# A state recurrence and a dense feed-forward layer on one core: 512 instead of 256 tokens per step of the layer

## The chip, the core and the metric

The kernel runs on one core of a Trainium2 chip. The core has a matrix engine (TensorE, PE in the profile; PEld is its weight load), VectorE (DVE), ScalarE (ACT), GpSimd (POOL) and SyncE (SP), which here only issues DMAs. Each engine works through its own instructions in the order in which they were written; the engines wait for one another on semaphores. Matmuls write to PSUM, eight banks of 2 KB per partition; all else lies in SBUF or in memory (HBM). The metric is the device time of one execution in microseconds.

## What is computed

```python
def _attn_ref(r, k, v, w, a, b):            # 4 batches, 8 heads, 768 steps, 40 wide
    for t in range(S):
        y[:, :, t] = np.einsum('bhd,bhde->bhe', rt, state)
        Sa = np.einsum('bhde,bhe->bhd', state, at)
        state_decay = state * wt[:, :, None, :] - np.einsum('bhd,bhe->bhde', Sa, bt)
        state = state_decay + np.einsum('bhd,bhe->bhde', vt, kt)

def _moe_ref(x, w_in, w_out):               # x: 3072 tokens x 320; w_in 320 x 2048; w_out 2048 x 320
    h = x @ w_in
    sp = np.where(h > 20.0, h, np.log1p(np.exp(np.minimum(h, 20.0))))
    g = h * np.tanh(sp)
    return (g @ w_out).astype(np.float32)
```

The recurrence's output y, reordered to 3072 tokens of 320 numbers, is the x of the dense layer.

## The kernel before

The first part (`attention`) computes the recurrence in 12 chunks of 64 time steps. Each chunk gives 256 tokens, which go to memory as `yD`, together with a factor `pD`; a token's x is the product of the two. A step of a chunk has parts a, u, d, b and c for each of two groups g of heads; part a's products are L284, part b's L314 with a mask on VectorE (L316), part c's L334 and L339 with a VectorE update of the state (L342, L346) and a ScalarE copy of the result (L343).

The second part (`Mlp.run`) is the dense layer. It takes T = 256 tokens at a time, one chunk, in 12 rounds i. Both products are made exact enough by splitting each factor into a rounded part (xh, gh and the weights' w_ih, w_oh) and its remainder (xl, gl, w_il, w_ol), in the type fp32r:

- `load_x(i)`: eight DMAs from SyncE's queue (four of `yD` into xy, L472 and L475; four of `pD` into xp, L473 and L476), then VectorE multiplies the two (L565), ScalarE rounds (xh, L566), VectorE subtracts (xl, L567, and L568). xy and xp have one buffer each (NXP = 1), xh and xl two (NX = 2).
- `mlp1(i, q)`, q = 0..3: a quarter of the 2048 hidden rows, as two PSUM banks ph of 2 blocks of 128 rows x 256 tokens; each block takes eight matmuls (L583). ScalarE applies the activation to a bank (L585) and then rounds all four blocks (gh, L588), VectorE subtracts (gl, L589). Four banks hold ph (NH = 4).
- `mlp2(i, q)`: 24 matmuls of 320 columns (L603 to L605): for each of four blocks of hidden rows and two blocks of 128 tokens, three matmuls into the token block's PSUM bank po. After q = 3 ScalarE copies each po to SBUF (os, L609) and SyncE's queue stores it (L610). Two of the four po banks are in use in a round; os has two buffers.

`mlp2` runs three quarters behind `mlp1` (LAG = 3), so that TensorE alternates between 32 matmuls of the first product and 24 of the second. The second weight matrix is read and split (`cv_d`, `cv_m`, `cv_w`: L453 to L463, L494, L495) in eight parts, three before the dense layer and five (`third`) after its first quarter.

The order of each engine's instructions is made by a list scheduler from priorities. It lets the dense layer's first instructions slip in between the last two steps of the recurrence (chunks 10 and 11), where TensorE would wait.

Of the kernel before, what the change touches and what calls it, by code (L numbers as in the profile page):

```python
# [7 lines left out]
F32 = mybir.dt.float32  # L8
F32R = mybir.dt.float32r
AF = mybir.ActivationFunctionType  # L10
# [33 lines left out]
def at(tc, k):  # L44
    return tc.high_priority(offset=OFF[k]) if OFF.get(k) else nullcontext()
# [33 lines left out]
def attention(ctx, tc, I, yD, pD, nch, M):  # L79
# [143 lines left out]
    def post_inv(n, TT, T1):  # L223
        gp = GP[n]
        for h in range(2):
            with at(tc, 'T%d' % h):
                px = ps_a.tile([64, 16, 32], F32, name="pa")
# [200 lines left out]
NHB = 3  # L428
NGB = 6
# [49 lines left out]
class Mlp:  # L479
# [70 lines left out]
    def run(self, nsc):  # L550
        tc, nc, W, yD, pD, out = self.tc, self.tc.nc, self, self.yD, self.pD, self.out
        V, A, PE, SP, G = nc.vector, nc.scalar, nc.tensor, nc.sync, nc.gpsimd
        T = 256
        ps_h, mpa = self.ps_h, self.mpa
        mp = self.pool("mp", 2, "left")
        ps_o = self.pool("ps_o", 8 - NH, "left", space=PSUM)

        def load_x(i):
            y = self.mpx.tile([128, 3, T], F32, name="xy", bufs=NXP)
            p = self.mpx.tile([128, 3, T], F32, name="xp", bufs=NXP)  # L560
            load_yp(nc, i, yD, pD, y, p, True)

            xh = self.mpx.tile([128, 3, T], F32R, name="xh", bufs=NX)
            xl = self.mpx.tile([128, 2, T], F32R, name="xl", bufs=NX)
            V.tensor_tensor(out=y, in0=y, in1=p, op=ALU.mult)  # L565
            A.copy(xh, y)  # L566
            V.tensor_tensor(out=xl, in0=y[:, 0:2], in1=xh[:, 0:2].bitcast(F32), op=ALU.subtract)  # L567
            V.tensor_tensor(out=xh[64:128, 2], in0=y[64:128, 2], in1=xh[64:128, 2].bitcast(F32), op=ALU.subtract)  # L568
            return xh, xl

        def mlp1(q, xh, xl):
            g = mpa.tile([128, 4, T], F32, name="g", bufs=NHB)
            for f0 in (0, 2):
                ph = ps_h.tile([128, 2, T], F32, name="ph")
                for j in range(2):
                    f = slice((f0 + j) * 128, (f0 + j) * 128 + 128)
                    o = ph[:, j]

                    for n, (w, x) in enumerate(((W.ih[q][:, 0, f], xh[:, 0]), (W.ih[q][:, 0, f], xl[:, 0]),
                                                (W.ih[q][:, 1, f], xh[:, 1]), (W.ih[q][:, 1, f], xl[:, 1]),  # L580
                                                (W.il[q][:, 0, f], xh[:, 0]), (W.il[q][:, 1, f], xh[:, 1]),
                                                (W.ih[q][:, 2, f], xh[:, 2]), (W.il[q][:, 2, f], xh[:, 2]))):
                        PE.matmul(o, w, x, start=(j == 0 and n == 0), stop=(n == 7), skip_group_check=True)  # L583

                A.activation(g[:, f0:f0 + 2], ph, AF.Mish)  # L585
            gh = mp.tile([128, 4, T], F32R, name="gh", bufs=NGB)
            gl = mp.tile([128, 4, T], F32R, name="gl", bufs=NGB)
            A.copy(gh, g)  # L588
            V.tensor_tensor(out=gl, in0=g, in1=gh.bitcast(F32), op=ALU.subtract)  # L589
            return gh, gl  # L590

        pos = {}

        def mlp2(i, q, gh, gl):
            if q == 0:
                pos[i] = [ps_o.tile([128, 320], F32, name="po") for _ in range(2)]
            po = pos[i]
            for j in range(4):
                f = q * 4 + j
                for k in range(2):  # L600
                    t = slice(k * 128, k * 128 + 128)
                    oh, ol = (w[f // 2][:, f % 2 * 320:f % 2 * 320 + 320] for w in (W.oh, W.ol))
                    PE.matmul(po[k], gh[:, j, t], oh, start=(f == 0), stop=False, skip_group_check=True)  # L603
                    PE.matmul(po[k], gh[:, j, t], ol, start=False, stop=False, skip_group_check=True)  # L604
                    PE.matmul(po[k], gl[:, j, t], oh, start=False, stop=(f == 15), skip_group_check=True)  # L605
            if q == 3:
                for k in range(2):
                    o = mp.tile([128, 320], F32, name="os")
                    A.copy(o, po[k])  # L609
                    SP.dma_start(out=out[i * T + k * 128:i * T + k * 128 + 128], in_=o)  # L610

        wait = []
        x = load_x(0)
        for i in range(nsc):
            for q in range(4):
                wait.append((i, q) + mlp1(q, *x))
                if (i, q) == (0, 0):
                    self.third()
                if q == 1 and i + 1 < nsc:
                    nx = load_x(i + 1)  # L620
                if len(wait) > LAG:
                    mlp2(*wait.pop(0))
            x = nx
        for w in wait:
            mlp2(*w)
# [32 lines left out]
```

## Time and profile before

| | us |
|---|---|
| median of 3 runs (lowest to highest) | 829.57 (829.17 to 835.69) |
| the profiled execution | 826.83 |
| its span, first to last instruction | 825.1 |
| TensorE busy in the span | 724.1 (88%) |
| VectorE, ScalarE, GpSimd busy | 461.1, 428.6, 103.2 |

The span is the profiled execution without some 1.7 us around it. Busy shares are means over two very different parts: a recurrence up to about 478 us, where the engines wait for each other, and the dense layer behind it. A row of a timeline gives the start, the duration, the engine, the line, the operation with its output and inputs, and in brackets how long the engine stood idle before it and who released it. A matmul's duration contains its way through the array, which overlaps the next one; how fast matmuls follow one another is read from their starts.

### The profile page before, as it was taken

The numbers are of one execution on the slowest core, as the hardware profiler recorded it, in microseconds if no ns is written. First come the engines' busy times: TensorE is split into PE (matmuls) and PEld (weight loads), VectorE is DVE, ScalarE is ACT, GpSimd is POOL, SyncE is SP. The second block draws the span as 40 slices with busy tenths as digits, with TensorE's granted clock in tenths as the row PEclk, the third lists the DMA queues.
The fourth block names the chain that finished last, engine by engine and source line by source line (L and its number), as shares of the span: only waits on it lengthen the run. The fifth ranks groups of instructions, "written<-read, shape, count | busy, mean of one in ns | idle before, by whom it ended". The sixth has DMA issues, their size and how long they took to land.

```text
span 825.1 us, 18795 instructions
## 1 busy us (share of the span) xinstructions
PE 724.1 (88%) x7816; PEld 679.3 (82%) x7816; DVE 461.1 (56%) x975; ACT 428.6 (52%) x937; POOL 103.2 (13%) x182
## 2 busy tenths in 40 slices
PE   2544798999789889889886999999999999999998
PEld 1433687788788788778775899999999999999998
DVE  6789979748989758889846456222222122122110
ACT  5534658775485866666784556233333333333331
POOL 8100021223222023221102100000000000000000
PEclk9767889999989999999999999999999999999999
DMA  6522323334433233423328543121121112000000
GB/s 174 143 73 65 96 54 73 93 82 111 106 84 81 60 97 103 92 74 111 105 92 191 130 139 99 39 56 33 23 55 37 36 39 55 18 20 17 17 1 33
DMA packets 58213, 61.92 MB, mean 75 GB/s; under 512 B 25536, under 2 KB 48704, under 8 KB 58128
## 3 DMA queue, kind: packets, MB, share of 16 engines
q1 hardware_dynamic: 49296, 40.94, 17.7%
q0 software_dynamic: 8832, 19.79, 9.9%
q8 instruction: 61, 1.00, 0.5%
q14 instruction: 24, 0.20, 0.1%
HBM read 48.79 MB, written 11.86 MB: 74 GB/s over the span
## 4 chain that ended last, share of the span: by engine, by line
PE 51%; ACT 9%; DVE 8%; DMA 4%; issue 2%; SPq 0%; DVEq 0%; ACTq 0%
PE ph L583 21%; PE po L604 7%; PE po L605 7%; PE po L603 7%; PE pa L258 3%; DMA cv_d<-in_wo 2%; PE pa L186 2%; DVE tmp L214 1%; DVE XL L216 1%; ACT bdT L249 1%; ACT bdT L250 1%; PE pq L314 1%; ACT KT L260 1%; PE pu L284 1%; DMA cv_d<-in_wi 1%
## 5 line engine op out<-in xcount | busy, mean ns | idle before, releaser
L583 PE MATMUL ph<-xh,w_ih 128*128 128x256 f32 x576 | 148.3, 283 | 3.1 <-ACT xh L566 3.1
L585 ACT ACTIVATE g<-ph 128x512 f32<-128x512 f32 x96 | 57.3, 598 | 180.0 <-PE ph L583 179.9
L589 DVE TENSOR_TENSOR gl<-g,gh 128x1024 fp32r<-128x1024 f32 x48 | 58.6, 1225 | 159.1 <-ACT gh L588 158.8
L583 PE MATMUL ph<-xh,w_il 128*128 128x256 f32 x576 | 123.7, 283 | 0.0
L186 PE MATMUL pa<-bk,ad 128*128 128x168 f32 x384 | 80.6, 359 | 45.5 <-DVE bk L170 15.0
L604 PE MATMUL po<-w_ol,gh 128*128 128x320 f32 x384 | 118.7, 309 | 0.1
L605 PE MATMUL po<-w_oh,gl 128*128 128x320 f32 x384 | 118.4, 309 | 0.0
L603 PE MATMUL po<-w_oh,gh 128*128 128x320 f32 x384 | 117.9, 309 | 0.0
L583 PEld LDWEIGHTS ph<-xh,w_ih 128*128 128x128 f32 x576 | 109.3, 190 | 3.4 <-ACT xh L566 3.4
L186 PEld LDWEIGHTS pa<-bk,ad 128*128 128x128 f32 x384 | 67.0, 222 | 50.8 <-issue 22.8
L583 PE MATMUL ph<-xl,w_ih 128*128 128x256 f32 x384 | 100.9, 284 | 0.0
L583 PEld LDWEIGHTS ph<-xh,w_il 128*128 128x128 f32 x576 | 96.2, 190 | 0.1
L583 PEld LDWEIGHTS ph<-xl,w_ih 128*128 128x128 f32 x384 | 73.1, 190 | 0.5 <-issue 0.3
L604 PEld LDWEIGHTS po<-w_ol,gh 128*128 128x128 f32 x384 | 72.1, 188 | 0.5 <-DVE w_ol L495 0.5
L605 PEld LDWEIGHTS po<-w_oh,gl 128*128 128x128 f32 x384 | 72.1, 188 | 0.1
L603 PEld LDWEIGHTS po<-w_oh,gh 128*128 128x128 f32 x384 | 71.8, 188 | 0.2
L216 DVE TENSOR_TENSOR XL<-XL,tmp 128x30 f32<-128x30 f32 (+9 forms) x180 | 59.0, 328 | 2.4
L214 DVE TENSOR_TENSOR tmp<-XL 128x30 f32<-128x30 f32 (+9 forms) x180 | 58.6, 325 | 2.3
L258 PE MATMUL pa<-bdT,HA 128*104 128x128 f32 x384 | 52.3, 291 | 6.9 <-ACT bdT L251 5.7
L258 PEld LDWEIGHTS pa<-bdT,HA 128*104 128x104 f32 x384 | 47.3, 182 | 10.6 <-ACT bdT L251 7.4
L314 PE MATMUL pq<-bdr,UVT 128*128 128x128 f32 x384 | 53.7, 285 | 0.3 <-DVE UVQ L316 0.2
L588 ACT CAST gh<-g 128x1024 fp32r<-128x1024 f32 x48 | 50.1, 1048 | 1.1
(89 smaller groups left out, 1219.6 us busy)
## 6 DMA issues: line engine op xcount, KB each, us to landing
wa<-in_wa SPq DMA_DIRECT2D x48, 162.5 KB
bk<-in_bk SPq DMA_DIRECT2D x48, 160.0 KB
cv_d<-in_wi SPq DMA_DIRECT2D x12, 512.0 KB
cv_d<-in_wo SPq DMA_DIRECT2D x8, 640.0 KB
pD<-P POOLq DMA_DIRECT2D x48, 81.2 KB, 2.2
VS<-in_vN POOLq DMA_DIRECT2D x24, 160.0 KB, 3.5
UVT<-in_vD POOLq DMA_DIRECT2D x24, 160.0 KB, 4.4
bdr<-in_rD POOLq DMA_DIRECT2D x24, 160.0 KB, 4.4
```

The source lines that it names most:

```text
L186: PE.matmul(pt[:, j], ad[:, s0 + j].rearrange("p k a t -> p (k a t)"), bk[:, s0 + j], start=(j == 0), stop=True, skip_group_check=True)
L214: V.tensor_tensor(out=tv, in0=X[:, i + 1:32, i:i + 1].broadcast_to([128, 31 - i, i]), in1=X[:, i:i + 1, 0:i].broadcast_to([128, 31 - i, i] ...
L216: V.tensor_tensor(out=X[:, i + 1:32, 0:i], in0=X[:, i + 1:32, 0:i], in1=tv, op=ALU.add)
L258: PE.matmul(pk[:, j], ha[:, s0 + j], bd[:, s0 + j].rearrange("p a t -> p (a t)"), start=(j == 0), stop=True, skip_group_check=True)
L314: PE.matmul(pq[:, s], UVT[:, g * 4 + s, be * 128:be * 128 + 128], br[:, be, g * 4 + s].rearrange("p a t -> p (a t)"), start=(s == 0), stop ...
L583: PE.matmul(o, w, x, start=(j == 0 and n == 0), stop=(n == 7), skip_group_check=True)
L585: A.activation(g[:, f0:f0 + 2], ph, AF.Mish)
L588: A.copy(gh, g)
L589: V.tensor_tensor(out=gl, in0=g, in1=gh.bitcast(F32), op=ALU.subtract)
L603: PE.matmul(po[k], gh[:, j, t], oh, start=(f == 0), stop=False, skip_group_check=True)
L604: PE.matmul(po[k], gh[:, j, t], ol, start=False, stop=False, skip_group_check=True)
L605: PE.matmul(po[k], gl[:, j, t], oh, start=False, stop=(f == 15), skip_group_check=True)
```

## The change

T becomes 512: a round i of the dense layer takes two chunks, and there are six rounds of eight steps q (`range(nsc // 2)`, `range(8)`). Line numbers behind the load move by one or two (L583 becomes L584, L585 L586, L609 L610, L565 L567).

- `load_x` issues the DMAs of two chunks (16) into tiles of twice the width, and then one multiply, one rounding and two subtractions on twice the columns.
- `mlp1` computes an eighth of the hidden rows: two blocks of 128 rows, each a bank ph of 512 tokens by eight matmuls of 512 columns. g, gh and gl keep their size (2 x 512 in place of 4 x 256).
- `mlp2` takes two blocks of hidden rows and four token blocks: again 24 matmuls of 320 columns, into four po banks at once. All four banks are in use in a round, and at its end four po are copied through the two os buffers.
- The second product needs one part of the split second weight matrix per step, where it needed two.

```diff
--- before.py
+++ after.py
@@ -550,7 +550,7 @@
     def run(self, nsc):
         tc, nc, W, yD, pD, out = self.tc, self.tc.nc, self, self.yD, self.pD, self.out
         V, A, PE, SP, G = nc.vector, nc.scalar, nc.tensor, nc.sync, nc.gpsimd
-        T = 256
+        T = 512
         ps_h, mpa = self.ps_h, self.mpa
         mp = self.pool("mp", 2, "left")
         ps_o = self.pool("ps_o", 8 - NH, "left", space=PSUM)
@@ -558,7 +558,9 @@
         def load_x(i):
             y = self.mpx.tile([128, 3, T], F32, name="xy", bufs=NXP)
             p = self.mpx.tile([128, 3, T], F32, name="xp", bufs=NXP)
-            load_yp(nc, i, yD, pD, y, p, True)
+            for c in range(2):
+                t = slice(c * 256, c * 256 + 256)
+                load_yp(nc, 2 * i + c, yD, pD, y[:, :, t], p[:, :, t], True)
 
             xh = self.mpx.tile([128, 3, T], F32R, name="xh", bufs=NX)
             xl = self.mpx.tile([128, 2, T], F32R, name="xl", bufs=NX)
@@ -569,22 +571,21 @@
             return xh, xl
 
         def mlp1(q, xh, xl):
-            g = mpa.tile([128, 4, T], F32, name="g", bufs=NHB)
-            for f0 in (0, 2):
-                ph = ps_h.tile([128, 2, T], F32, name="ph")
-                for j in range(2):
-                    f = slice((f0 + j) * 128, (f0 + j) * 128 + 128)
-                    o = ph[:, j]
-
-                    for n, (w, x) in enumerate(((W.ih[q][:, 0, f], xh[:, 0]), (W.ih[q][:, 0, f], xl[:, 0]),
-                                                (W.ih[q][:, 1, f], xh[:, 1]), (W.ih[q][:, 1, f], xl[:, 1]),
-                                                (W.il[q][:, 0, f], xh[:, 0]), (W.il[q][:, 1, f], xh[:, 1]),
-                                                (W.ih[q][:, 2, f], xh[:, 2]), (W.il[q][:, 2, f], xh[:, 2]))):
-                        PE.matmul(o, w, x, start=(j == 0 and n == 0), stop=(n == 7), skip_group_check=True)
-
-                A.activation(g[:, f0:f0 + 2], ph, AF.Mish)
-            gh = mp.tile([128, 4, T], F32R, name="gh", bufs=NGB)
-            gl = mp.tile([128, 4, T], F32R, name="gl", bufs=NGB)
+
+            g = mpa.tile([128, 2, T], F32, name="g", bufs=NHB)
+            for j in range(2):
+                ph = ps_h.tile([128, T], F32, name="ph")
+                f = slice((q % 2 * 2 + j) * 128, (q % 2 * 2 + j) * 128 + 128)
+                h, l = W.ih[q // 2], W.il[q // 2]
+
+                for n, (w, x) in enumerate(((h[:, 0, f], xh[:, 0]), (h[:, 0, f], xl[:, 0]), (h[:, 1, f], xh[:, 1]),
+                                            (h[:, 1, f], xl[:, 1]), (l[:, 0, f], xh[:, 0]), (l[:, 1, f], xh[:, 1]),
+                                            (h[:, 2, f], xh[:, 2]), (l[:, 2, f], xh[:, 2]))):
+                    PE.matmul(ph, w, x, start=(n == 0), stop=(n == 7), skip_group_check=True)
+
+                A.activation(g[:, j], ph, AF.Mish)
+            gh = mp.tile([128, 2, T], F32R, name="gh", bufs=NGB)
+            gl = mp.tile([128, 2, T], F32R, name="gl", bufs=NGB)
             A.copy(gh, g)
             V.tensor_tensor(out=gl, in0=g, in1=gh.bitcast(F32), op=ALU.subtract)
             return gh, gl
@@ -593,30 +594,30 @@
 
         def mlp2(i, q, gh, gl):
             if q == 0:
-                pos[i] = [ps_o.tile([128, 320], F32, name="po") for _ in range(2)]
+                pos[i] = [ps_o.tile([128, 320], F32, name="po") for _ in range(4)]
             po = pos[i]
-            for j in range(4):
-                f = q * 4 + j
-                for k in range(2):
+            for j in range(2):
+                f = q * 2 + j
+                oh, ol = (w[f // 2][:, f % 2 * 320:f % 2 * 320 + 320] for w in (W.oh, W.ol))
+                for k in range(4):
                     t = slice(k * 128, k * 128 + 128)
-                    oh, ol = (w[f // 2][:, f % 2 * 320:f % 2 * 320 + 320] for w in (W.oh, W.ol))
                     PE.matmul(po[k], gh[:, j, t], oh, start=(f == 0), stop=False, skip_group_check=True)
                     PE.matmul(po[k], gh[:, j, t], ol, start=False, stop=False, skip_group_check=True)
                     PE.matmul(po[k], gl[:, j, t], oh, start=False, stop=(f == 15), skip_group_check=True)
-            if q == 3:
-                for k in range(2):
+            if q == 7:
+                for k in range(4):
                     o = mp.tile([128, 320], F32, name="os")
                     A.copy(o, po[k])
                     SP.dma_start(out=out[i * T + k * 128:i * T + k * 128 + 128], in_=o)
 
         wait = []
         x = load_x(0)
-        for i in range(nsc):
-            for q in range(4):
+        for i in range(nsc // 2):
+            for q in range(8):
                 wait.append((i, q) + mlp1(q, *x))
                 if (i, q) == (0, 0):
                     self.third()
-                if q == 1 and i + 1 < nsc:
+                if q == 3 and i + 1 < nsc // 2:
                     nx = load_x(i + 1)
                 if len(wait) > LAG:
                     mlp2(*wait.pop(0))
```

How this moves instructions is shown at three places. In all of them ph, xh, xl, w_ih and w_il are the tiles of the first product; pu, pq, KT, VS, UVQ, ST and bkn are those of the recurrence.

TensorE, before, where the first matmuls of the dense layer stand: in part c of chunk 10, between the two halves of group 0 (L334, L339).

```order
L334 MATMUL pq<-UVQ_119,bkn 64x104
L334 MATMUL pq<-UVQ_120,bkn 64x104
L339 MATMUL pq<-bdr_121,smd 64x2x64 x4
L583 MATMUL ph<-xh,w_ih_927 128x256 x2
L583 MATMUL ph<-xh,w_ih_5064 128x256 x2
L334 MATMUL pq<-UVQ_119,bkn 64x104
```

TensorE, after, at the first matmuls of the dense layer: they stand behind all of chunk 10's part c and just ahead of chunk 11's part a for group 1 (L284, L304).

```order
L334 MATMUL pq<-UVQ_120,bkn 64x104
L339 MATMUL pq<-bdr_121,smd 64x2x64 x4
L584 MATMUL ph<-xh,w_ih_927 128x512 x4
L284 MATMUL pu<-KT,VS_116 64x64
L304 MATMUL pu<-cst,ST_123 128x128 x4
L284 MATMUL pu<-KT,VS_116 64x64 x7
L284 MATMUL pu<-KT,VS_117 64x64 x8
L584 MATMUL ph<-xl,w_ih_927 128x512
L584 MATMUL ph<-xh,w_ih_927 128x512
L584 MATMUL ph<-xl,w_ih_927 128x512
```

So the first matmuls of the dense layer move behind three halves of part c and one part a, and four of them stand ahead of the other part a.

VectorE, before, around the multiply of the first x (L565), in part c of chunk 10: the state updates L342 and the split of the second weight matrix (cv_w, w_ol) follow it.

```order
L316 TENSOR_TENSOR UVQ_119<-pq,cst 128x8x64
L461 TENSOR_SCALAR cv_w<-cv_m 128x640
L565 TENSOR_TENSOR xy<-xy,xp 128x768
L462 SCALAR_TENSOR_TENSOR cv_w<-cv_m,cv_w 128x640
L342 TENSOR_TENSOR stn<-ST_122,pq 128x160
L463 SCALAR_TENSOR_TENSOR cv_w<-cv_d,cv_w 128x640
L567 TENSOR_TENSOR xl<-xy,xh 128x512
L568 TENSOR_TENSOR xh<-xy,xh 64x256
L495 SCALAR_TENSOR_TENSOR w_ol_5371<-cv_w,w_oh_5370 128x640
L342 TENSOR_TENSOR stn<-ST_122,pq 128x160
```

VectorE, after, at the same multiply (L567 now), first place: it stands between the two updates (L342) of group 1's state ST_123.

```order
L346 TENSOR_TENSOR ST_122<-stn,R 128x8x40
L495 SCALAR_TENSOR_TENSOR w_ol_5371<-cv_w,w_oh_5370 128x640
L342 TENSOR_TENSOR stn<-ST_123,pq 128x160
L567 TENSOR_TENSOR xy<-xy,xp 128x1536
L342 TENSOR_TENSOR stn<-ST_123,pq 128x160
L346 TENSOR_TENSOR ST_123<-stn,R 128x8x40
L569 TENSOR_TENSOR xl<-xy,xh 128x1024
```

VectorE, after, at the multiply of the second x: it stands between the third and the fourth mask product (L316) of chunk 11's part b.

```order
L316 TENSOR_TENSOR UVQ_120<-pq,cst 128x8x64
L316 TENSOR_TENSOR UVQ_119<-pq,cst 128x8x64
L567 TENSOR_TENSOR xy<-xy,xp 128x1536
L316 TENSOR_TENSOR UVQ_120<-pq,cst 128x8x64
L569 TENSOR_TENSOR xl<-xy,xh 128x1024
L570 TENSOR_TENSOR xh<-xy,xh 64x512
L590 TENSOR_TENSOR gl<-g,gh 128x1024 x4
```

What moved: both multiplies are twice as wide, and an instruction of the recurrence that the next matmuls need now stands right behind each.

ScalarE, before, at the end of a round, with the semaphores that each instruction waits for (DMAHW: a DMA; 49 is only a label): two copies of po to os between two roundings and activations.

```order
L588 CAST gh<-g 128x1024 [waits Activation_49]
L609 COPY os<-po 128x320 [waits DMAHW1_49,PE_49]
L609 COPY os<-po 128x320 [waits DMAHW2_49,PE_49]
L585 ACTIVATE g<-ph 128x512 [waits DVE_49,PE_49]
L585 ACTIVATE g<-ph 128x512 [waits PE_49]
L566 CAST xh<-xy 128x768 [waits DMAHW5_49,DMAHW6_49,DMAHW4_49,DMAHW3_49]
```

ScalarE, after, at the end of a round: four copies, the third and the fourth of which wait for a DMA more.

```order
L589 CAST gh<-g 128x1024 [waits Activation_49]
L610 COPY os<-po 128x320 [waits PE_49] x2
L610 COPY os<-po 128x320 [waits DMAHW5_49,PE_49,Activation_49]
L586 ACTIVATE g<-ph 128x512 [waits DVE_49,PE_49]
L610 COPY os<-po 128x320 [waits DMAHW6_49,Activation_49]
L586 ACTIVATE g<-ph 128x512 [waits PE_49]
L589 CAST gh<-g 128x1024 [waits Activation_49]
```

What moved: the third copy stands ahead of the next activation (L586) and waits until the first copy's buffer has been stored; the fourth stands behind that activation.

## Rows read from the trace of the kernel before

**Rows 1.** The page's head and TensorE's line; share of the span in brackets.

```profile
span 825.1 us, 18795 instructions
...
PE 724.1 (88%) x7816; PEld 679.3 (82%) x7816; DVE 461.1 (56%) x975; ACT 428.6 (52%) x937; POOL 103.2 (13%) x182
```

**Rows 2.** TensorE by stretch: window, its length, busy us (matmuls), granted clock, DMA share, GB/s.

```profile
391.10:394.50 3.40, 1.70 (x49) 0.96 0.48 144
394.50:397.90 3.40, 3.40 (x19) 0.54 0.80 199
447.15:450.28 3.13, 0.00 (x0) 1.00 0.41 105
450.28:475.00 24.72, 24.00 (x287) 1.00 0.54 131
525.00:800.00 275.00, 275.00 (x2098) 1.00 0.11 30
```

**Rows 3.** Chain that ended last, in time: start us, us, engine, tile, line, count.

```profile
439.86 7.25 DMA cv_d<-in_wo
...
464.53 5.98 DMA xy<-yD
470.63 0.96 DVE xy L565
471.59 0.61 DVE UVQ L316
...
516.80 3.83 PE ph L583 x32
...
803.72 3.83 PE ph L583 x32
```

**Rows 4.** Timeline, lead-in: start us, us, engine, line, operation [idle before <-releaser].

```profile
446.54 0.61 PE L339 MATMUL pq<-bdr,smd 128*64 128x128 f32 x8
447.19 0.77 ACT L459 ACTIVATE cv_m<-cv_d 128x640 f32<-128x640 f32 x1 [4.46 <-DMA cv_d<-in_wo]
...
450.28 0.74 PE L583 MATMUL ph<-xh,w_ih 128*128 128x256 f32 x4 [3.14 <-ACT xh L566]
...
455.92 0.33 PE L284 MATMUL pu<-KT,VS 104*64 104x64 f32 x2 [0.54 <-ACT VS L277]
...
457.84 0.38 PE L583 MATMUL ph<-xh,w_ih 128*128 128x256 f32 x1
...
458.74 0.93 PE L334 MATMUL pq<-UVQ,bkn 128*64 128x104 f32 x16
...
459.94 0.88 PE L334 MATMUL pq<-UVQ,bkn 128*64 128x104 f32 x16
```

**Rows 5.** Groups by line and shape from 470 us: busy us, mean ns, idle before.

```profile
L589 DVE TENSOR_TENSOR gl<-g,gh 128x1024 fp32r<-128x1024 f32 x48 | 58.6, 1225 | 159.1 <-ACT gh L588 158.8
...
L588 ACT CAST gh<-g 128x1024 fp32r<-128x1024 f32 x48 | 50.1, 1048 | 1.1
L609 ACT COPY os<-po 128x320 f32<-128x320 f32 x24 | 10.2, 426 | 29.1 <-PE po L605 28.9
L565 DVE TENSOR_TENSOR xy<-xy,xp 128x768 f32<-128x768 f32 x10 | 9.6, 958 | 30.3 <-DMA xy<-yD 30.3
L566 ACT CAST xh<-xy 128x768 fp32r<-128x768 f32 x10 | 8.3, 826 | 3.2 <-PE ph L583 3.2
```

**Rows 6.** Timeline, the last microseconds.

```profile
821.23 0.86 ACT L609 COPY os<-po 128x320 f32<-128x320 f32 x2 [11.96 <-PE po L605]
821.32 0.31 PE L605 MATMUL po<-w_oh,gl 128*128 128x320 f32 x1
821.68 0.81 SPq L610 DMA_DIRECT2D out<-os  x2
```

**Rows 7.** Timeline of SyncE's queue where a pair of blocks is stored.

```profile
803.76 0.81 SPq L610 DMA_DIRECT2D out<-os  x2
```

**Rows 8.** DMA busy tenths from 803 to 806.2 us, 40 slices of 0.08 us.

```profile
DMA  0000000000000000000079999699999630009000
```

## The prediction

> **What bounds the kernel now.** I read the page first: TensorE is busy for 88% of the span [rows 1]. That is a mean, so I read TensorE by stretch: from 525 to 800 us it is busy for 275.00 of 275 us at the full clock (1.00, the 2.4 GHz level), so nothing but its own pace matters there; before that it has gaps, 3.13 us without one matmul from 447.15 to 450.28 and 0.72 us from there to 475 [rows 2]. The chain of waits gives the pace: blocks of 32 matmuls L583 begin at 516.80 and, 39 rounds later, at 803.72, and one lasts 3.83 us [rows 3]. A round is 286.92 / 39 = 7.357 us; 32 matmuls of 256 columns take 3.83, 119.7 ns each; the 24 of 320 columns take the other 3.53, 147.0 ns each. Third, the timeline of the lead-in shows why TensorE waits: its first L583 at 450.28 was held 3.14 us by ScalarE's rounding of x [rows 4]. The end is copies, stores and the close of the program, 825.1 - 821.63 = 3.5 us behind the last matmul, which ends at 821.32 + 0.31 [rows 1, 6].
>
> **The first product.** The change replaces 12 x 4 x 32 = 1536 matmuls of 256 columns by 768 of 512; the 1152 of the second product stay. The 64 columns between the two forms take 27.3 ns, 0.43 ns each, about one cycle of the 2.4 GHz level. At a column a cycle 256 columns are 106.7 ns and 320 are 133.3; the measured paces stand 13.0 and 13.7 ns above, so a matmul costs its columns plus some 13.3 ns that do not grow with them. 512 columns then cost 213.3 + 13.3 = 226.7 ns, two of before 239.4: 12.7 x 768 = 9.8 us less. The straight line through the two paces (0.427 ns a column) gives 228.9 ns and 8.1 us. No 512 column matmul is in the trace, so the bounds: in proportion to the 320 column row, 235.2 ns, 3.2 us less; with the fixed part gone, 213.3 ns, 20.0 us less. I take 9.8, since 256 and 320 columns show the same remainder.
>
> The Trainium skill, page "TensorE: Matmul & The Clock Gate", section "Back-to-back issue gap", gives N / 2.4 + 2.5 ns for an isolated stream at full clock, 215.8 ns for 512 columns; the sum would then be 18.1 us less for this term. The same section puts a stream with weight loads at some 131 ns for 512 columns; this trace disagrees, with 147.0 ns for 320.
>
> **The other engines in a round** do the same work on tiles of the same size (activation, rounding gh, subtraction gl, 24 copies of po in all), and the loads are joined in pairs. They lie beside TensorE: 275 us of matmuls without a gap [rows 2]. Were that cover gone, the joined multiply would cost 1.8 us a round.
>
> **The lead-in** loses. By the order, the first matmuls stand behind three half parts c and a part a of the recurrence; before, the dense layer filled the waits between these. I walk it with durations of the rows. TensorE is free at 446.54 + 0.61 = 447.15. A half part c takes 1.20 us (458.74 to 459.94), a part a 1.92 (455.92 to 457.84) [rows 4]. The eight further DMAs of x queue behind a weight load of 7.25 us that was issued at 439.86 [rows 3], so x is there at 451 to 452 by estimate; but VectorE comes to its multiply only at about 453.0, since the weight split ahead of it starts from ScalarE's cv_m at 447.19 [rows 4] and L461 to L463, L495 and three state updates follow. The multiply: 958 ns for 768 columns and 1225 for 1024 [rows 5] make 1.04 ns a column, 1.77 us for 1536, done at 454.8. The rounding: 826 and 1048 ns [rows 5] make 1.48 us; ScalarE comes to it behind two recurrence copies at 455.8, so the first dense matmul runs at 457.3 and not at 450.28. In these 10.15 us TensorE has 3 x 1.20 + 1.92 = 5.5 us of work: 4.65 idle. Then part a of group 1 waits 0.8 us more, for copies that stand behind the rounding and one cv_m on ScalarE. Last, in part b of chunk 11 the fourth mask product stands behind the multiply of the second x. Its buffers come free at 454.8 (xp) and about 459.9 (xy, when L570 has read it); before, the xy load took 5.98 us from issue to its end [rows 3]; with twice as many DMAs I put the landing at 469, multiply and mask product (1.77 and 0.61) at 471.4, and TensorE arrives at about 470.8: 0.7 idle. Together 6.2 against 3.85 before [rows 2], a loss of 2.4 us. Bounds: 0, if TensorE never waits for either multiply beyond the 3.85 of before; 6, if the second x lands 2.7 us later and the clock falls as below.
>
> **The end** loses too. Four po are copied through two os buffers, so the third copy waits until the first is stored. po[0] is complete nine matmuls ahead of the end E (1.32 us), copies take 0.43 us [rows 5], so the first store is issued at E - 0.87. Before, a pair of stores issued at 803.76 had moved its bytes by 805.6, the first half by about 805.15 [rows 7, 8]: 1.4 us, and the notice of it comes later; from the second store's issue to the close of the program 825.1 - 822.1 = 3.0 us pass [rows 6]. I take 2.2, between the two: third copy from E + 1.35, fourth to E + 2.2, where the last copy ended at E + 0.46 (822.09) before: 1.7 us more. Bounds 0.9 (store 1.4) and 2.5 (store 3.0).
>
> **Between rounds** the same chain is hidden. The next round writes po[0] again after an eighth of the first product, 16 x 0.227 = 3.63 us behind the last matmul of its predecessor, po[3] at 4.95 us. The third copy ends at 1.8, one activation of some 0.6 us stands between, the fourth ends at about 2.8: 2.1 us to spare, five times. The cover is that eighth; without it each handover costs some 3 us.
>
> **The second weights** are needed half as fast, one part a step; what TensorE lost for that before is under 1 us, and I count nothing.
>
> **Sum:** -9.8 + 2.4 + 1.7 = -5.7 us. The span goes from 825.1 to 819.4, the profiled execution from 826.83 to 821.1. The median shown stands 2.7 us above that execution; 829.57 - 5.7 = 823.9.
>
> **The rivals.**
> - *The fixed part goes at 512 columns.* A matmul would cost its columns alone, 213.3 ns: 768 x 13.3 = 10.2 us less again, 813.7. For it: nothing in the trace says what the 13 ns are. Against: it is the same at 256 and at 320 columns, where the stream had already grown by 27 ns. The sameness at two widths makes me give this little. By the 2.5 ns of the Trainium skill (page "TensorE: Matmul & The Clock Gate", section "Back-to-back issue gap") this case would end at 815.6.
> - *The remainder grows with the columns* (235.2 ns): 6.6 us of the gain are gone, 830.5. For it: 13.7 is a little above 13.0. Against: in proportion to 256 columns, 320 would take 149.6 and not 147.0.
> - *The lead-in is worse.* The last load of the second x is issued near 465.7 and takes the 5.98 us of before: multiply and mask product end at 474.1, 2.6 us more idle. TensorE's thinner lead-in may also cost clock: from 394.50 to 397.90 the granted clock was 0.54, behind a stretch with 1.70 of 3.40 us busy; yet it stayed at 1.00 across the gap at 447.15 [rows 2]. Half speed for 3.4 us costs 1.7. Together 828.2.
> - *The handover of po becomes the bound*, the one that ends slower. If a store takes S, the fourth copy ends S + 0.59 behind the round, and TensorE waits from S = 4.4 on. With 5.98, what a load took [rows 3]: 1.6 x 5 = 8.1, and 3.8 more at the end: 835.8. From S = 4.95 on the kernel is slower than before. For it: four banks and two buffers leave no slack elsewhere. Against: the DMA share in the dense part is 0.11 [rows 2], and a pair of stores moved its bytes in 1.9 us.
>
> **How the numbers follow.** The forecast 0.52 (its own range 820.5 to 827, from the straight line, a lead-in of 0 to 5 and an end of 0.9 to 2.5); fixed part gone 0.11; remainder in proportion 0.09; lead-in worse 0.20; handover 0.08. Range 818 to 832: it leaves out the fixed part gone and the handover, 0.19. One per cent, 8.3 us, is about what a measurement here tells from no change: faster is below 821.3, slower above 837.9. Faster: 0.11 and the lower part of the forecast, 0.12: 0.23. Slower: the worse half of the handover, with something for lead-ins that are worse still: 0.05. Within: 0.72.
>
> **What would show it.** In the dense part a step should last 16 x 0.227 + 3.53 = 7.16 us and TensorE have no gaps; L584 starts should be 227 ns apart. The first L584 should start near 457, the recurrence's last matmul end near 474 (478 before), the fourth copy at the end about 2 us behind the last matmul. I am wrong if the starts are 216 or 235 ns apart, if a gap stands ahead of po's first matmul of a round, or if TensorE idles over 10 us from 447 to 475.

## The result, and the profile after

The changed kernel takes 824.05 us, median of 6 runs (822.15 to 827.21), beside 834.01 us for the kernel before in the same comparison: 0.9883 of it, 95% interval [0.9846, 0.9919]. Two later comparisons gave 0.9872 [0.9832, 0.9911] and 0.9844 [0.9795, 0.9893]. The forecast was 823.9 us and "within one per cent" the likeliest; the time came out to 0.2 us, but the kernel is 1.2 to 1.6% faster, just beyond that bound. The sum gave -5.7 us; the comparisons show -10 to -13 (1.2 to 1.6%). The base was as much too low as the gain: the median of the three runs shown was 829.57 us, that of 57 later runs of the same kernel is 835.8 (826.8 to 843.6).

The page's head and TensorE's line after, for [rows 1]:

```profile
span 821.8 us, 17217 instructions
PE 722.7 (88%) x7048; PEld 644.8 (78%) x7048; DVE 458.7 (56%) x957; ACT 428.7 (52%) x931; POOL 103.4 (13%) x182
```

TensorE by stretch after, in the windows of [rows 2] (length, busy us, matmuls, granted clock, DMA share, GB/s):

```profile
447.15:450.28 3.13, 2.16 (x32) 1.00 1.07 252
450.28:475.00 24.72, 20.57 (x224) 0.93 0.75 149
525.00:800.00 275.00, 275.00 (x1536) 1.00 0.09 25
```

The dense part still has no gap. The chain of waits after (start, us, tile, line, count), for [rows 3]:

```profile
540.94 3.65 PE ph L584 x16
544.59 0.15 PE po L604
...
548.11 3.65 PE ph L584 x16
```

A step (16 matmuls L584, 24 of the second product) lasts 548.11 - 540.94 = 7.17 us, and there are 48; before there were 48 of 32 and 24 matmuls that lasted 7.357 us each [rows 3]. Of the 16 dense starts in a step, twelve are 226 to 227 ns apart, the first three 231 to 235 and the last 237.

The lead-in after, for [rows 4] (VectorE, ScalarE and TensorE; in brackets the idle time before, and what ended it):

```profile
451.31 0.49 DVE L461 TENSOR_SCALAR cv_w<-cv_m 128x640 int32<-128x640 int32 x1 [3.47 <-ACT cv_m L459]
451.72 0.68 DVE L316 TENSOR_TENSOR UVQ<-pq,cst 128x512 f32<-128x512 f32 x1
...
457.33 1.76 DVE L567 TENSOR_TENSOR xy<-xy,xp 128x1536 f32<-128x1536 f32 x1 [1.37 <-DMA xp<-pD]
```

```profile
450.51 0.77 ACT L459 ACTIVATE cv_m<-cv_d 128x640 f32<-128x640 f32 x1 [5.61 <-DMA cv_d<-in_wo]
...
459.12 1.47 ACT L568 CAST xh<-xy 128x1536 fp32r<-128x1536 f32 x1 [0.96 <-DVE xy L567]
```

```profile
452.46 0.94 PE L334 MATMUL pq<-UVQ,bkn 128*64 128x104 f32 x16 [3.15 <-DVE UVQ L316]
...
460.65 1.56 PE L584 MATMUL ph<-xh,w_ih 128*128 128x512 f32 x4 [1.97 <-ACT xh L568]
```

Two waits, 3.15 + 1.97 = 5.1 us. The longer one is not the one forecast: VectorE has an instruction of the weight split (L461) ahead of the recurrence's fourth mask product (L316); it waits for ScalarE's cv_m, and that for a weight load that lands at 450.5. SyncE's queue issued that load here, between loads of x:

```profile
444.03 0.52 SPq L453 DMA_DIRECT2D cv_d<-in_wo  x1
```

That is 4.2 us later than before (439.86 [rows 3]). The recurrence itself was 2.2 us later in this trace (first L316 at 445.2, 443.0 before). From issue to cv_m the load took 6.5 us, before 7.3. The same load stands behind the 3.14 us of before, where VectorE (this is the kernel before) went from it to the multiply that the rounding of x waits for:

```profile
448.00 0.49 DVE L461 TENSOR_SCALAR cv_w<-cv_m 128x640 int32<-128x640 int32 x1 [2.32 <-ACT cv_m L459]
448.41 0.95 DVE L565 TENSOR_TENSOR xy<-xy,xp 128x768 f32<-128x768 f32 x1
```

Behind the two waits of the changed kernel the granted clock falls (TensorE, columns as in [rows 2]):

```profile
454.00:461.00 7.00, 5.03 (x86) 1.00 0.49 117
461.00:468.00 7.00, 7.00 (x52) 0.76 1.13 233
```

0.76 over 7 us is 3.4 us at the lower level, 0.50 (461.3 to 464.7), some 1.7 us of work lost.

The end after, for [rows 6] (ScalarE, then SyncE's queue, then TensorE):

```profile
815.63 0.86 ACT L610 COPY os<-po 128x320 f32<-128x320 f32 x2 [11.08 <-PE po L606]
817.98 0.91 ACT L610 COPY os<-po 128x320 f32<-128x320 f32 x2 [1.48 <-DMA out<-os]
```

```profile
816.08 3.17 SPq L611 DMA_DIRECT2D out<-os  x4
```

```profile
816.60 0.31 PE L606 MATMUL po<-w_oh,gl 128*128 128x320 f32 x1
```

The last matmul ends at 816.91, the fourth copy 1.98 us later, the program 4.9 us later (3.5 before, [rows 6]).

### The profile page after: what moved, and what is told of

Read it like the earlier page. It is cut to its first block, busy times and chain, and to the rows that moved or that the text cites. A ratio compares the mean times of both kernels' runs of the same rounds, so it can differ in the third digit from the quotient of the medians.

```text
span 821.8 us, 17217 instructions
## 1 busy us (share of the span) xinstructions
PE 722.7 (88%) x7048; PEld 644.8 (78%) x7048; DVE 458.7 (56%) x957; ACT 428.7 (52%) x931; POOL 103.4 (13%) x182
## 4 chain that ended last, share of the span: by engine, by line
PE 52%; ACT 9%; DVE 7%; DMA 3%; issue 2%; SPq 0%; ACTq 0%; DVEq 0%
PE ph L584 21%; PE po L605 7%; PE po L604 7%; PE po L606 7%; PE pa L258 2%; PE pa L186 2%; DMA xp<-pD 1%; DVE tmp L214 1%; DVE XL L216 1%; PE pq L314 1%; ACT bdT L249 1%; PE pu L284 1%; ACT bdT L250 1%; DMA cv_d<-in_wi 1%; ACT KT L260 1%
## 5 line engine op out<-in xcount | busy, mean ns | idle before, releaser
L586 ACT ACTIVATE g<-ph 128x512 f32<-128x512 f32 x96 | 57.3, 598 | 180.5 <-PE ph L584 180.3
L186 PE MATMUL pa<-bk,ad 128*128 128x168 f32 x384 | 85.6, 376 | 42.8 <-DVE bk L170 15.0
L584 PE MATMUL ph<-xh,w_ih 128*128 128x512 f32 x288 | 112.7, 393 | 2.0 <-ACT xh L568 2.0
L186 PEld LDWEIGHTS pa<-bk,ad 128*128 128x128 f32 x384 | 71.5, 235 | 48.2 <-issue 22.8
L584 PE MATMUL ph<-xh,w_il 128*128 128x512 f32 x288 | 97.1, 391 | 0.0
L584 PE MATMUL ph<-xl,w_ih 128*128 128x512 f32 x192 | 75.1, 391 | 0.0
L584 PEld LDWEIGHTS ph<-xh,w_ih 128*128 128x128 f32 x288 | 54.1, 188 | 12.1 <-ACT xh L568 2.2
L584 PEld LDWEIGHTS ph<-xh,w_il 128*128 128x128 f32 x288 | 54.0, 188 | 11.6 <-issue 0.2
L258 PEld LDWEIGHTS pa<-bdT,HA 128*104 128x104 f32 x384 | 46.7, 179 | 11.1 <-ACT bdT L251 7.2
L334 PE MATMUL pq<-UVQ,bkn 128*64 128x104 f32 (+1 forms) x768 | 44.7, 254 | 7.8 <-DVE UVQ L316 5.5
```

Source lines behind the costliest of these rows:

```text
L186: PE.matmul(pt[:, j], ad[:, s0 + j].rearrange("p k a t -> p (k a t)"), bk[:, s0 + j], start=(j == 0), stop=True, skip_group_check=True)
L258: PE.matmul(pk[:, j], ha[:, s0 + j], bd[:, s0 + j].rearrange("p a t -> p (a t)"), start=(j == 0), stop=True, skip_group_check=True)
L584: PE.matmul(ph, w, x, start=(n == 0), stop=(n == 7), skip_group_check=True)
L586: A.activation(g[:, j], ph, AF.Mish)
```

## The experiments

A trace that is read here is one execution, and in one kernel the time of the recurrence (up to 445 us) differs from execution to execution, since the granted clock falls to half at other places (shown below). So I read each trace from the first mask product of chunk 10 (the first L316 in the lead-in) to the last matmul's end, and sum the time from each matmul's start to the next by product:

| kernel | first L316 | last matmul ends | between | first product | second product | TensorE idle in the lead-in |
|---|---|---|---|---|---|---|
| before | 443.0 | 821.6 | 378.6 | 186.2 | 169.5 | 3.9 |
| before, second trace | 456.2 | 833.4 | 377.2 | 186.7 | 169.4 | 1.7 |
| changed | 445.2 | 816.9 | 371.7 | 176.4 | 168.7 | 5.1 |
| changed, second trace | 452.6 | 824.2 | 371.6 | 176.0 | 168.7 | 5.4 |
| changed, third trace | 455.1 | 821.1 | 365.9 | 176.0 | 168.7 | 1.0 |
| two of 256 | 449.8 | 824.7 | 374.9 | 184.9 | 168.8 | 1.0 |
| bf16 | 453.9 | 820.7 | 366.8 | 164.8 | 178.3 | 3.4 |
| four os, second run | 453.4 | 822.3 | 368.8 | 176.0 | 168.7 | 3.7 |
| one os | 457.2 | 824.8 | 367.7 | 176.2 | 170.0 | 1.0 |
| x first | 455.9 | 829.7 | 373.9 | 180.2 | 171.1 | 4.4 |
| slices, x first, four os | 454.3 | 829.4 | 375.2 | 182.6 | 168.8 | 3.4 |
| one weight later, four os | 448.6 | 818.5 | 369.9 | 176.0 | 168.7 | 4.8 |

### The width alone

```diff
-                    PE.matmul(ph, w, x, start=(n == 0), stop=(n == 7), skip_group_check=True)
+                    for c0, c1 in ((0, 256), (256, 512)):
+                        PE.matmul(ph[:, c0:c1], w, x[:, c0:c1], start=(n == 0 and c0 == 0), stop=(n == 7), skip_group_check=True)
```

> The changed kernel with each 512 column matmul of the first product issued as two of 256 columns; all else stays, the pairing of chunks and the four accumulators too. Fixed part per matmul (13.3 ns): 768 more matmuls at 240.0 against 226.7 ns a pair, +10.2 us against the changed kernel, about 834; starts 120.0 ns apart. Remainder in proportion to columns: +0 to 3 us. If the gain came from the pairing of steps and not from the width, within 2 us of the changed kernel.

Measured: 839.36 us, 1.0046 of before [1.0014, 1.0078]; some 15 us above the changed kernel of the same comparison (824.57), 10.2 expected. The chain of this kernel, in its dense part:

```profile
527.23 3.84 PE ph L585 x32
534.58 3.83 PE ph L585 x32
```

The step is back at 7.35 us, and the first product takes 184.9 us against 176.0: 8.9 us are the width's, shown with all else kept. The other 6 us of the difference do not show in its trace, which is of the fastest of its twelve executions (831.70 us).

### What the fixed part is

```diff
+                    wb = w.bitcast(mybir.dt.bfloat16).rearrange("p (c two) -> p c two", two=2)[:, :, 1]
+                    xb = x.bitcast(mybir.dt.bfloat16).rearrange("p (c two) -> p c two", two=2)[:, :, 1]
-                    PE.matmul(ph, w, x, start=(n == 0), stop=(n == 7), skip_group_check=True)
+                    PE.matmul(ph, wb, xb, start=(n == 0), stop=(n == 7), skip_group_check=True)
```

> The changed kernel with the first product's matmuls reading the upper 16 bits of the same values as bf16 (the product is then less exact; number, order and shapes of the matmuls stay). If the 13.3 ns beside the columns belong to every matmul, starts stay 226.7 ns apart and the dense part keeps its length. If they belong to the fp32r form, starts come 213 to 220 ns apart, 5 to 10 us less from the 768. By the Trainium skill, page TensorE: Matmul & The Clock Gate, section Back-to-back issue gap, it would be 215.8 ns.

Measured (one run): 827.7 us. The chain:

```profile
531.39 3.62 PE ph L586 x16
```

3.62 against 3.65 us for 16: within a step the starts are 224 to 226 ns apart. What the bf16 stream saves where it hands over (a start after 26 ns) the second product gives back (its first matmul then takes 353): both together 343.1 us against 344.8. So the 13 ns are not the fp32r form's alone; the weight load takes 96 ns here and not 188, so they are not the load's length either. The bf16 values are read in place, each the upper half of a 4 byte number; no run reads them packed.

> The changed kernel with each 512 column matmul issued as one of 384 and one of 128 columns. If the fixed 13.3 ns stand beside any width, a pair takes 173.3 + 66.7 = 240.0 ns, as two of 256 do, and the dense part is 10.2 us longer than the changed kernel's. If something else sets a floor for a short matmul (its weight load lasts 188 ns in the trace, beside the matmul ahead of it), 128 columns take up to 100 ns more: a pair up to 340 ns, up to 87 us longer.

```diff
-                    for c0, c1 in ((0, 256), (256, 512)):
+                    for c0, c1 in ((0, 384), (384, 512)):
```

Measured (one run): 876.27 us; the chain:

```profile
534.51 4.53 PE ph L585 x32
```

16 pairs in 4.53 us, 283 ns a pair and not 240: neither end of what I expected. Within a pair the short matmul starts 228 ns behind the long one, and the next long one 58 ns behind the short one. 13.3 ns beside the columns hold from 256 to 512 columns and not with a 128 column matmul in each pair; why is not shown.

### The end and the handover of po

```diff
-                    o = mp.tile([128, 320], F32, name="os")
+                    o = mp.tile([128, 320], F32, name="os", bufs=4)
```

> The changed kernel with four os buffers in place of two. Theory (the end alone pays for two buffers): the last copy ends 0.46 us behind the last matmul, where it ended 1.98 us behind it; -1.5 us, about 822.5, and nothing in the middle, where the wait of 1.5 us lies beside TensorE's work. Rival (the waits between rounds cost as well): up to 5 x 1.5 us more, about 815.

> Four os buffers again: the last copy 0.5 us behind the last matmul and 3.5 us from the last matmul to the close, against 4.9; 1.5 us below the changed kernel of the same call.

Measured: 821.72 us, 0.9833 [0.9783, 0.9883], then 828.08 us, 0.9888 [0.9845, 0.9932], beside 824.57 and 823.96 for the changed kernel. The time doesn't resolve it. The trace does (the second of the two; ScalarE and TensorE at the end):

```profile
820.97 1.75 ACT L610 COPY os<-po 128x320 f32<-128x320 f32 x4 [11.08 <-PE po L606]
```

```profile
821.95 0.31 PE L606 MATMUL po<-w_oh,gl 128*128 128x320 f32 x1
```

The copies end at 822.72, 0.46 us behind the last matmul, the span (825.8) 3.5 us behind it: the end's 1.4 us are the two buffers', and the dense part is unchanged to 0.1 us.

> The changed kernel with one os buffer: each copy of po waits for the store before it, 1.9 us from issue to the next copy in the first profile. At the end the fourth copy ends 6.3 us behind the last matmul (1.98 with two buffers), +4.3 us. Between rounds the fourth copy would end some 7 us behind the round, and po[3] is wanted 4.95 us behind it, or 6.1 us where five dense matmuls are moved ahead of it: theory, 1 to 2 us of wait five times, together +9 us (833), with gaps of TensorE at each round's first po[3]. Rival (the handover has more room than I counted): +4.3 us alone, 828.4.

```diff
-                    o = mp.tile([128, 320], F32, name="os")
+                    o = mp.tile([128, 320], F32, name="os", bufs=1)
```

Measured: 831.97 us, 0.9958 [0.9929, 0.9988], 7.4 us above the changed kernel, between the rival's +4.3 and the theory's +9. From the last matmul to the close it takes 833.9 - 824.8 = 9.1 us, 4.2 more; and those who waited for the copies of po are, in the listing of line L610:

```profile
  PEld po L604: 1.2, 5
```

five waits, 1.2 us together and not 5 to 10: the scheduler moved dense matmuls ahead of the late po, and a handover has that room. With two buffers the fourth copy of a round ends here (ScalarE of the changed kernel):

```profile
539.65 0.86 ACT L610 COPY os<-po 128x320 f32<-128x320 f32 x2 [0.52 <-PE po L606]
542.01 0.43 ACT L610 COPY os<-po 128x320 f32<-128x320 f32 x1 [1.49 <-DMA out<-os]
...
543.30 0.42 ACT L610 COPY os<-po 128x320 f32<-128x320 f32 x1
```

and po[3] is written from 545.75 on (three matmuls of 147 ns for each block from 544.43): 2.0 us to spare.

### The lead-in: a second trace of each kernel

> The kernel before, once more, for a second trace of it. Its first L316 stood at 113.0 us in its first trace and the one of the halves at 113.1, while three kernels with 512 columns stood at 117.8 to 118.4, with code that is the same up to there. If that goes with the kernel, 113 us again; if it is chance of the granted clock, any time from 113 to 118. The dense part must repeat: a step of 7.36 us, last L316 group to the end 353.6 us.

> The changed kernel unchanged, run beside the others as their basis. Theory (a 512 column matmul every 226.7 ns, 768 of them in place of 1536 at 120.0): 5 to 10 us below the kernel before, near 824 us. If the granted clock falls in the lead-in again (in the first profile a stretch near 460 us stood at 0.66), it belongs to the new lead-in; if it does not, it was chance.

> The changed kernel a third time, beside the two that follow and for a third trace of its lead-in. Its two traces show 5.1 and 5.4 us of idle TensorE there, with the clock full until about 461 us; the kernels with only the end changed (one or four os buffers) show 1.0 us each, with the clock at half for 7 to 10 us ahead of it. Theory: the recurrence's own pace decides, so 1 us of idle if the clock falls between 440 and 460, 5 if not. Time again about 824.5.

Measured: before 838.61 us (one run); the changed kernel 824.57, 0.9872 [0.9832, 0.9911], and 823.96, 0.9844 [0.9795, 0.9893]. The listing of L316 in the lead-in, of before's first and second trace (ns min/median/max, first and last start):

```profile
L316 DVE TENSOR_TENSOR UVQ<-pq,cst x4: 685/692/693, 443.0 to 453.1; 128x512 f32<-128x512 f32 x4
```

```profile
L316 DVE TENSOR_TENSOR UVQ<-pq,cst x3: 691/692/692, 456.2 to 458.7; 128x512 f32<-128x512 f32 x3
```

One kernel, 13 us apart ahead of anything that the change touches. TensorE by stretch in the two traces, columns as in [rows 2], shows what differs:

```profile
29.00:113.00 84.00, 49.10 (x428) 0.74 0.27 77
113.00:440.00 327.00, 287.74 (x4306) 0.98 0.36 94
```

```profile
29.00:113.00 84.00, 51.43 (x360) 0.63 0.27 76
113.00:440.00 327.00, 290.98 (x4275) 0.96 0.34 89
```

The granted clock is 0.63 and not 0.74 in the first stretch, 0.96 and not 0.98 in the second; in the second trace it is also at its lower level from 447.4 to 457.7, where the first trace has 1.00. So the guess that the early start goes with the kernel fell: it varies within one kernel, and the first trace of before is an early one. The third trace of the changed kernel shows what that does to the lead-in:

```profile
447.00:454.00 7.00, 6.18 (x51) 0.50 1.09 248
454.00:461.00 7.00, 7.00 (x93) 0.95 1.01 176
461.00:468.00 7.00, 5.97 (x85) 1.00 0.64 167
```

The clock is at its lower level (1.2 GHz, 0.50) in 447 to 454 us, the recurrence is late, and the loads (the sixteen of x issued from 444.2 to 458.4, in the second trace, at the full clock, from 444.8 to 460.2) are no longer behind it: x's multiply (L567) waits 0.17 us for its load and not 1.37, and TensorE idles 1.0 us and not 5.1. Where two such traces are compared, before (second) and changed (third), the stretch from the first L316 to the last matmul is 377.2 against 365.9: -11.3 us. The first product gives 10.6 of it and the second 0.7; with +1.4 at the close, -9.9, at the lower edge of what the comparisons show. Where the clock was full up to 461 us, the first traces, it is 378.6 against 371.7: -6.9, with the close -5.5.

The fall of the clock behind the lead-in's waits came again in the second trace of the changed kernel: 5.4 us idle, then the lower level from 461.7 to 465.2. So two of its two traces with the clock full up to there have it; the trace of before has a wait of 3.14 us [rows 4] and no fall, and neither has the last kernel below (4.8 us idle, 1.00 throughout). The theory for the third trace (1 us idle where the clock falls between 440 and 460 us, 5 where not) held for the three traces of this kernel, but not for all: with four os the clock was at half from 445.9 to 452.7, and 3.7 us of idle stayed.

### The lead-in: an earlier x

```diff
             for c in range(2):
-                t = slice(c * 256, c * 256 + 256)
-                load_yp(nc, 2 * i + c, yD, pD, y[:, :, t], p[:, :, t], True)
+              with tc.high_priority(offset=600) if i == 0 else nullcontext():
+                t = slice(c * 256, c * 256 + 256)
+                load_yp(nc, 2 * i + c, yD, pD, y[:, :, t], p[:, :, t], True)
```

> The changed kernel with the first x's sixteen loads issued with a higher priority, ahead of the weight load that stood among them; the scheduler then puts four dense matmuls ahead of chunk 10's last part c. Theory (the lead-in's idle is the late x): landing some 3 us earlier (the weight load moves 640 KB, 3.8 us of all engines by its packets in the first trace), first dense matmul 3 us earlier against the recurrence, TensorE's idle in the lead-in 2 to 4 us less and the total 2 to 4 us less. Rival (the idle is the recurrence's own waits and the multiply and rounding): no change in the idle beyond 1 us.

Measured: 835.55 us, 1.0020 [0.9982, 1.0058], by the ratios 1.4 to 1.8% above the changed kernel and not below it. Its dense matmuls do come earlier, and are then interleaved with the recurrence's part c (TensorE):

```profile
475.54 0.51 PE L585 MATMUL ph<-xl,w_ih 128*128 128x512 f32 x1
475.97 0.43 PE L339 MATMUL pq<-bdr,smd 128*64 128x128 f32 x2
476.33 0.50 PE L585 MATMUL ph<-xh,w_ih 128*128 128x512 f32 x1
...
501.21 0.41 PE L605 MATMUL po<-w_oh,gh 128*128 128x320 f32 x1 [2.51 <-ACT gh L590]
```

One dense and two recurrence matmuls take 476.33 - 475.54 = 0.79 us here. A dense matmul in a stream takes 0.23; the 24 matmuls of a half part c took 1.20 us [rows 4], so two take 0.10. Going to and fro once thus costs about 0.45 us; there are seven more such turns in this lead-in than in the changed kernel's, and seventeen more in the next kernel's. And the recurrence's last matmul starts 39.4 us behind the first L316 (27.8 in the changed kernel's third trace), and the second product waits for what follows it, by ScalarE's rounding of gh:

```profile
500.11 2.94 ACT L590 CAST gh<-g 128x1024 fp32r<-128x1024 f32 x3 [4.16 <-DMA yD<-yev]
```

It waits for the recurrence's last output to be stored. Why it should (gh may lie in memory that this frees) was only argued, not shown. Against the changed kernel's third trace the first product takes 4.1 us more and the second 2.3, waits included; to the last matmul it is 373.9 against 365.9, 7.9 us more. Behind its waits of 2.51 and 0.41 us the clock falls here too, from 503.3 to 506.7. Seven turns (3.2), the two waits (2.9) and 3.4 us at half the clock (1.7) make 7.8. The first x did come earlier: its first dense matmul stands 7.9 us behind the first L316, 11.1 there. That gain was worth less than what the new order cost.

The kernel with more of this (x in three slices of rows, each multiplied and rounded by itself, p loaded in rows of 1040 bytes, x first, four os) was to gain too. Of its edit only the loop over the slices is shown:

```diff
+            for k in range(3):
+                yk = y[:, k].rearrange("p (s t) -> p s t", t=64)
+                V.tensor_tensor(out=yk, in0=yk, in1=p[:, k].rearrange("p (s t) -> p s t", t=65)[:, :, 0:64], op=ALU.mult)
+                A.copy(xh[:, k], y[:, k])
```

> Three edits on the changed kernel: four os buffers (-1.5 us at the end); x multiplied, rounded and split by its three slices of rows, so that the first dense matmul waits for a third of that work (-2 us in the lead-in); p loaded in rows of 1040 bytes in place of pieces of 256, and the first x ahead of the weights. Theory: TensorE's idle from the lead-in's start falls from 5.1 us to 2 or less, total -4 to -6 us against the changed kernel, 818 to 820. If the clock falls in the lead-in again, 1.7 us less gain. Rival (the early dense matmuls only delay the recurrence, whose waits come back later): -1.5 us alone.

Measured: 832.18 us, 0.9977 [0.9946, 1.0009], 1.0 to 1.4% above the changed kernel. Its first dense matmul comes 4.8 us behind the first L316, its first product takes 6.5 us more than in the changed kernel's third trace, and the recurrence's last matmul starts 44 us behind its first L316. The rival named there (early dense matmuls delay the recurrence, whose waits come back later) came true, and cost more than it said.

```diff
-NO1 = 3
+NO1 = 2
```

> Four os buffers, and one of the three second weights that are loaded in the lead-in moved to those loaded later. Theory (the weight split and its 640 KB load delay x and the fourth mask product): up to 2 us less idle in the lead-in where the clock is full, so 0 to 2 us below the kernel with four os buffers alone. Rival (the second product then waits for the moved weight): a gap ahead of the second product as in the kernel with the first x ahead of the weights (2.5 us), 1 to 3 us above it.

Measured (with four os): 825.44 us, 0.9850 [0.9808, 0.9892], beside 823.96 for the changed kernel and 828.08 for four os alone: no difference that can be told. Its trace, with the clock full, has 4.8 us of idle in the lead-in, 3.55 of them at the fourth mask product again, which waits for cv_m as in the changed kernel: one weight load stays among the loads of x. No version was shown to be faster than the changed kernel.

## Why the prediction was right, and where it was not

- **What bounds the kernel.** Right: 275.00 of 275 us busy before and after.
- **First product, -9.8.** Mechanism right, -8.9 by the width alone. 226.7 ns is the spacing of twelve starts in sixteen; the first three and the last of a step are 4 to 10 ns longer, which the sum took for none. The straight line's 228.9 ns was closer to the mean. The rival in which the fixed part goes is refuted (it would be 213.3), and so is the remainder in proportion (235.2).
  The Trainium skill, page "TensorE: Matmul & The Clock Gate", section "Back-to-back issue gap", gives N / 2.4 + 2.5 ns for an isolated matmul at full clock, 215.8 at 512 columns. No stream here shows it: 226.7 in fp32r, 224 to 226 in bf16.
- **Lead-in, +2.4.** This term failed. In the first trace its size was about right: up to the first dense matmul TensorE idled 5.1 us, 4.65 forecast. But 3.15 of them stand at chunk 10's fourth mask product and 1.97 at the first dense matmul, and the forecast's two later waits, 0.8 and 0.7 us, did not come: the second x cost nothing. The first dense matmul started at 460.65 and the recurrence's last matmul at 478.8, not near 457 and 474.
  The walk had kept ScalarE's cv_m at its time of before, 447.19 [rows 4]; it came at 450.51, since its load was issued 4.2 us later, half of that because the recurrence itself was late in this trace. Its transfer was no longer than before here (6.5 us to cv_m), but 9.6 in the second trace, where TensorE waited 4.4 us for that mask product. And the weight split (L461), which the walk saw only ahead of the multiply, stands ahead of the mask product too. x itself landed near 457 and not at 451 to 452: its last load was issued only at 451.24, with the DMA engines full (share 1.07, before 0.41 [rows 2]). The sum also left out the fall of the clock behind these waits, 1.7 us, which the rival "the lead-in is worse" had.
  And the whole term comes and goes between executions of one kernel. In the changed kernel's third trace it is gone (1.0 us idle), and against before's second trace there is a gain: the first product takes 1.7 us less than the width explains (186.7 against 184.9 for two of 256), and TensorE waits 0.7 us less. A part of the 1.7 may be that the matmuls follow in fewer pieces between the recurrence's (6 before, 5 in two of 256, 4 in the changed kernel); that is argued, not shown.
- **The end, +1.7.** Right: +1.4, gone with four os. A store holds its buffer 1.9 us (issue 816.08, third copy 817.98), 2.2 forecast.
- **Between rounds, hidden, 2.1 us to spare.** Right: 2.0, and no gap. The rival that ends slower needed a store of 4.4 us.
- **Second weights, nothing.** Nearly: 0.7 us gained in the second product.
- **The base.** The sum was made against a trace at the low edge of what this kernel does (826.83), and set on a median of three; that the forecast met 824.05 is luck, two errors of some 5 us, in the gain and in the base, against each other. The chances (0.23 for faster by over 1%) carried the same mistake.

Span and mean granted clock are known of every execution, so the kernels can be compared at one clock. A straight line of span against clock, with one slope for all kernels, puts the spans at a clock of 0.95 at 833.3 us for before (57 executions) and 822.3 for the changed kernel (18): 10.9 us apart, 95% interval 9.7 to 12.1. That agrees with the later pair of traces (-9.9) and not with the first pair (-5.5) or the forecast (-5.7), so in most executions the lead-in seems to cost nothing. Against the changed kernel the same line gives one os +5.5 (its trace: 4.2 + 1.2), x first +8.3 (7.9) and the slices +8.2 (9.2 less 1.4 at the end), each to about 2 us.

What stays open: two of 256 stands at +11.9 there, and at 8.9 in its trace; four os at -1.2 and then +3.0, where -1.4 was expected. What the lead-in does in most executions rests on few traces, and these come from different chips.

## What to carry to other kernels

Where one engine is busy without gaps, its own spacing per instruction, read at two sizes, forecasts a third size to 1%; look at the starts that open and close a group too. A term that rests on a wait between an engine's work and a load holds for one relation of the two: take a second trace before counting it, above all if the granted clock falls ahead of that place, and ask whether the wait itself may cost clock. Give a change in percent against many runs of before, not against the trace that was read, and compare runs at the same granted clock.

## What the runs showed of the hardware

- Two 256 column matmuls take 240 ns, one of 384 and one of 128 take 283 for the same columns (full clock, fp32r, a weight load for each).
- A pair of the recurrence's plain fp32 matmuls (weights 64 wide) between two fp32r matmuls cost about 0.45 us each time beyond the two streams' own paces. Whether the type or the weights' shape makes it is not shown.
- Behind waits of 3.15 and 1.97 us (changed kernel), and of 2.51 and 0.41 us (x first), TensorE ran at 0.50 of its clock for 3.4 us; behind 3.14 us in the kernel before it did not.
- bf16 in place of fp32r made a 512 column matmul with its weight load 1 to 2 ns faster and no more, though the load itself took 96 ns in place of 188.
- The same program reached the same place of the recurrence at 443.0 and at 456.2 us, with a mean granted clock of 0.93 and 0.89 up to there; the traces show no other cause, and none was tested.
